# Sliding-window attention and a token/channel mixer on one core: the loads of v leave the place behind those of q and k and go behind the transposes of u

## The chip, the core and the metric

The kernel runs on one core of a Trainium2 chip. The core has five engines, each with a queue of its own that it works through in order: TensorE (matrix products, called PE in the profile), VectorE (DVE), ScalarE (ACT), GpSimd (POOL) and SyncE (SP, here used only to issue transfers). Sixteen DMA engines move data; the instructions that start them stand in the queues of SyncE, ScalarE and GpSimd. The metric is device time in microseconds of one execution, lower is better. Each number given for a kernel is the median of several runs.

## What is computed

Eight batches, eight heads, 576 positions, head size 64. Attention with a linear position bias and a causal window of 128, and then a mixer: two products over the positions, two over the channels.

```python
scores = scale * q @ k^T                      # (8, 8, 576, 576)
mask   = (rel >= 0) & (rel < 128)             # rel = query - key
scores = where(mask, scores - slope[h] * |rel|, -1e9)
x      = softmax(scores) @ v                  # heads side by side: (8, 576, 512)
h      = relu(x^T @ w_tok1) @ w_tok2          # over the 576 positions, width 256
u      = x + h^T
out    = u + relu(u @ w_ch1) @ w_ch2          # over the 512 channels, width 1536
```

Inputs and output are float32 in HBM; inside, the kernel works in bfloat16, and the loads that GpSimd issues cast on the way.

## The kernel before

The 576 positions of a batch are four chunks of 128 and a tail of 64; the tails of two batches are worked on together in the odd batch. Heads go in pairs. The work is cut into small functions with short names (lines 831 to 906), and the order in which they are issued is written out by hand in five strings. PROLOGUE, FIRST and SECOND cover the start and batches 0 and 1. PERIOD is issued for b = 2, 3, 4, 5 and 6, called rounds 2 to 6 here, and LAST for batch 7. A name with primes belongs to a later batch: S01'' in round b is a piece of batch b + 2. A name that a batch does not have is left out, so rounds 5 and 6 issue no loads of batch b + 3.

In a round the pieces are:

- `Lq'''`, `Lk'''`: loads of q and k of batch b + 3 into the buffers qn, qnt and kn, knt, five transfers each, issued by GpSimd (lines 188 to 211). There is one buffer for q and one for k, so a load waits until the transposes have read the batch before.
- `Zq''`, `Zk''`: DMA transposes of q and k of batch b + 2 from these buffers into qT and kT, two each, issued by SyncE (lines 217 to 221).
- `S..`: scores of eight blocks (six of batch b + 2 and two of b + 1): products on TensorE (lines 356 to 365), exponent on ScalarE (line 370), the product with the mask on VectorE (lines 376 to 385).
- `P0''` to `P4'`: probabilities times v on TensorE (lines 416 to 448), normalised by VectorE into x (lines 429 to 463).
- `v0'''` to `v4'''`: loads of v of batch b + 3 by GpSimd (line 213), into one of three buffers vp.
- `K`, `U`, `UT`: the two products over the positions, of batch b + 1 (lines 472 to 523); VectorE adds x and writes u (buffer ub, line 508).
- `X0'` to `X3'`: u turned. For batches 3 to 7 (`U_DMA`, line 19) X0 and X2 are DMA transposes of two chunks each on SyncE from ub into utb (lines 526 to 533), and X1 and X3 are empty. utb and ub have two buffers each.
- `C0` to `C11`: first product over the channels of batch b (line 548), which reads utb; `D..`: the second (line 607), each chunk added to u by VectorE (line 612) into one of four buffers ob and stored by SyncE (line 613). `T`, `E` and `Y` are the same for the tails, in odd batches.

The order around the change is thus set by three queues: GpSimd's, with Lq, Lk and v; SyncE's, with Zq, Zk, the stores and the X transposes; and TensorE's, which follows the string. In PERIOD the v loads stand between K0' and D20; as GpSimd has nothing else there, they are issued right after Lk'''.

Of the kernel before, what the change touches and what calls it, by code (L numbers as in the profile page):

```python
# [18 lines left out]
U_DMA = (3, 4, 5, 6, 7)  # L19
# [19 lines left out]
"""  # L39
PERIOD = """  # L40
Zq'' Lq''' C0 C7 T0 C6 C3 S31' S30' C4 P2' Zk'' Lk''' Y C10 C8 C9 P1' C2 T1 C1 P4' C11 P3' C5
K0' v4''' T2 K1' S01'' S00'' D00 v3''' v0''' D01 D02 U0' v1''' U3' UT' U2' U1' X1' P0'' v2'''
D20 D21 D10 X2' S10'' S11'' D11 X0' D22 D12 D30 D31 D32 S21'' S20'' X3' E0 E1 E2
"""
LAST = """
T1 C0 C1 T0 Y C11 C2 C10 T2 C7 C3 C8 C6 C5 C4 C9 D00 E0 D01 D02 E1 E2 D10 D30 D11 D20 D12 D31
# [16 lines left out]
def kernel(  # L63
# [11 lines left out]
    nc = tc.nc  # L75
    P = nc.NUM_PARTITIONS
# [6 lines left out]
    NC = S // P  # L83
# [11 lines left out]
    def T(name, shape, dt=bf16):  # L95
        return sb.tile(shape, dt, name=name, tag=name)
# [27 lines left out]
    i2 = T("i2", [P, ST])  # L124
    dist = T("dist", [P, 2, P], f32)
    distb = T("distb", [P, 2, P])
    sid = T("sid", [P, H, P])

    masks = T("masks", [P, 2, 2, 2, 2, P])
# [28 lines left out]
    utb = [T(f"utb{i}", [P, NC, NCB, P]) for i in range(2)]  # L158
# [54 lines left out]
    def load_v(b, c):  # L213
        t = vp[b % 3]
        load_tok(t[:, c, :, 0:D] if c < NC else None, t[0:ST, NC, :, 0:D], v, b, c)
# [188 lines left out]
    def pv(b, qb):  # L404
        vt = vp[b % 3]

        def f():
            psO = S2()
            for bank in range(2):
                o = psO[:, bank, :]  # L410
                first = True
                for hh in range(4):
                    h = bank * 4 + hh
                    ov = o[:, hh * (D + 1):(hh + 1) * (D + 1)]
                    if qb > 0:
                        nc.tensor.matmul(  # L416
                            ov, lhsT=prob(b, qb - 1, h, 1),
                            rhs=vt[:, qb - 1, h, 0:D + 1], start=first, stop=False)
                        first = False
                    nc.tensor.matmul(  # L420
                        ov, lhsT=prob(b, qb, h, 0),
                        rhs=vt[:, qb, h, 0:D + 1], start=first, stop=(hh == 3))
                    first = False
            ov = psO[:, :, 0:4 * (D + 1)].rearrange("p b (h e) -> p b h e", h=4)
            r = rt[qb % 2]
            rv = r[:, 0:H].rearrange("p (b h) -> p b h", b=2)

            def g():
                nc.vector.reciprocal(out=rv[:, :, :, None], in_=ov[:, :, :, D:D + 1])
                nc.vector.tensor_tensor(  # L430
                    out=xb[b % 2][:, qb, :].rearrange("p (b h d) -> p b h d", b=2, h=4),
                    in0=ov[:, :, :, 0:D],
                    in1=rv[:, :, :, None].broadcast_to([P, 2, 4, D]), op=ALU.mult)
            later(0, g)
        return f

    def pv_tail(b):
        vt = vp[b % 3]

        def f():  # L440
            psO = S2()
            E = 2 * (D + 1)
            for bank in range(2):
                for j in range(2):
                    hp = bank * 2 + j
                    o = psO[:, bank, j * E:(j + 1) * E]
                    for t in range(2):
                        nc.tensor.matmul(o, lhsT=prob_tail(b, t, hp),  # L448
                                         rhs=vt[:, NC - 1 + t, 2 * hp:2 * hp + 2, 0:D + 1],
                                         start=(j == 0 and t == 0), stop=(j == 1 and t == 1))  # L450

            def g():
                oa = psO[:, :, 0:2 * E].rearrange("p b (h e) -> p b h e", h=4)
                ra = rt[0][:, 0:H].rearrange("p (b h) -> p b h", b=2)
                nc.vector.reciprocal(out=ra[:, :, :, None], in_=oa[:, :, :, D:D + 1])
                for i in range(2):
                    ps = slice(i * D, (i + 1) * D)
                    ov = psO[ps, :, 0:2 * E].rearrange("p b (j i e) -> p b j i e", j=2, i=2)[:, :, :, i, :]
                    rv = rt[0][ps, 0:H].rearrange("p (b j i) -> p b j i", b=2, j=2)[:, :, :, i]
                    nc.vector.tensor_tensor(  # L460
                        out=xt[b % 2][ps, :].rearrange("p (b j i d) -> p b j i d", b=2, j=2, i=2)[:, :, :, i, :],
                        in0=ov[:, :, :, 0:D],
                        in1=rv[:, :, :, None].broadcast_to([D, 2, 2, D]), op=ALU.mult)
            later(0, g)
        return f
# [91 lines left out]
    def ch1_tail(b, g, n=4):  # L557
# [12 lines left out]
                                 func=ACT.Relu)  # L570
        return f

    def utail_trans(b):

        pi2 = (b // 2) % 2

        def f():
            nc.sync.dma_start_transpose(
                out=ut2[pi2][:, :, :], in_=utt[pi2][:, :, :, :].rearrange("p c i x -> p (c i x)"))
        return f  # L580
# [250 lines left out]
    def names(b):  # L831

        d = {}
        for kb in range(NC):
            for j in range(2):
                d[f"S{kb}{j}"] = score(b, kb, j)
        for qb in range(NC):
            d[f"P{qb}"] = pv(b, qb)
        d["P4"] = pv_tail(b)
        for i in range(2):  # L840
            d[f"K{i}"] = tok1(b, i)
        for c in range(NC):
            d[f"U{c}"] = tok2(b, c)
            d[f"X{c}"] = utrans(b, c)
        d["UT"] = tok2_tail(b)
        for ht in range(NHT):
            d[f"C{ht}"] = ch1(b, ht)
        if b % 2:
            for g in range(3):
                d[f"T{g}"] = ch1_tail(b, g)  # L850
            if b in Y_DMA:
                d["Y"] = utail_trans(b)
        for c in range(NC):
            for i, f in enumerate(ch2(b, c, CH2_PARTS)):
                d[f"D{c}{i}"] = f
        if b % 2:
            for i, f in enumerate(ch2_tail(b, CH2_PARTS)):
                d[f"E{i}"] = f
        for c in range(NC + 1):
            d[f"v{c}"] = lambda c=c: load_v(b, c)  # L860
        if b >= PE_BATCHES:
            d["Lq"], d["Lk"] = lambda: load_tokens(qn, qnt, q, b), lambda: load_tokens(kn, knt, k, b)
            d["Zq"] = lambda: dma_transpose(qT[b % 2], qn, qnt)
            d["Zk"] = lambda: dma_transpose(kT[b % 2], kn, knt)
        else:
            for nm, dst, src in (("q", qs, q), ("l", ks, k)):
                for hp in range(NHP):
                    d[f"{nm}{hp}"] = lambda dst=dst, src=src, hp=hp: load4(dst, src, b, hp)
                for hp in (0, 2):
                    d[f"{nm}{hp}{hp + 1}"] = lambda dst=dst, src=src, hp=hp: load4(dst, src, b, hp, 4)  # L870
            d["qt"] = lambda: load_qk_tail(b)
            for hp in range(NHP):
                d[f"A{hp}"] = pe_transpose(b, hp)
            d["AT"] = pe_transpose_tail(b)
        if b == 0:
            for hp in range(NHP):
                d[f"M{hp}"] = lambda hp=hp: mask_exps(hp)
                d[f"p{hp}"] = pv_hp(hp)
                d[f"k{hp}"] = tok1_hp(hp)
                d[f"u{hp}"] = tok2_hp(hp)  # L880
                d[f"x{hp}"] = utrans_hp(hp)
            for hp in range(2):
                d[f"q{hp}"] = lambda hp=hp: load_f32(nc.scalar, qf0, q, hp)
                d[f"l{hp}"] = lambda hp=hp: load_f32(nc.sync, kf0, k, hp)
                d[f"cq{hp}"] = lambda hp=hp: cast_f32(nc.vector.tensor_copy, qs, qf0, hp)
                d[f"ck{hp}"] = lambda hp=hp: cast_f32(nc.scalar.copy, ks, kf0, hp)
            d["LC"] = late_constants
            d["FC"] = first_constants
            d["e1"], d["e2"] = lambda: ones_v(1), lambda: ones_v(2)
            d["ek"], d["ex"] = fill_k1, fill_x1  # L890
            d["I"] = make_ident
            d["J"] = make_dist
            d["LW"] = load_w12
            d["B"] = make_bias
            d["O"] = lambda: ones_v(0)
            for kb in range(NC - 1):
                d[f"s{kb}"], d[f"t{kb}"] = score_half(kb, 0), score_half(kb, 1)
            for j in range(2):
                d[f"m{j}"] = lambda j=j: mask_tails(j)
            for g in range(3):  # L900
                d[f"G{g}"] = lambda g=g: load_wc1(g)
            for g in range(2):
                d[f"H{g}"] = lambda g=g: load_wc2(g)
            for n in range(1, 5):
                d[f"W{n}"] = warm(n)
        return d
# [46 lines left out]
```

The softmax here doesn't subtract the row's maximum and nothing guards it: scores larger than these inputs give would overflow.

## Time and profile before

| | us |
|---|---|
| median of 5 runs | 288.33 |
| lowest and highest of them | 287.83, 288.34 |
| the profiled execution's own time | 288.48 |
| its span, first to last instruction | 286.7 |
| TensorE busy (2535 products) | 280.4 (98%) |
| VectorE busy | 165.0 (58%) |
| ScalarE busy | 118.6 (41%) |
| GpSimd busy | 101.4 (35%) |

The busy time of TensorE is that of its matrix products; they are pipelined and their ends are modelled, so that a high share alone does not say that TensorE runs at its peak. Issuing a transfer occupies GpSimd for about 0.9 us for a load of four-dimensional shape such as v's; on SyncE such an issue is listed too, but is not counted as busy. The profile's table of DMA queues gives the share of the engines' time that the packets of a queue took: 81.9% for those that GpSimd issued over the whole span, 29.6% for those of SyncE. In a short stretch the sum of such shares can be above 1, since packets of several transfers are in flight together. From issue to landing a load of v takes 5.3 us (median), one of q or k 5.9, a transpose of u 3.3, the large one of q 3.9 and of k 3.8, and a store of line 613 2.1.

### The profile page before, as it was taken

What the parts mean: (1) busy time and instruction counts of PE and PEld (TensorE: products, weight loads), DVE (VectorE), ACT (ScalarE), POOL (GpSimd) and SP (SyncE); (2) the same over time, 40 slices, a digit from 0 to 9 for tenths busy, and PEclk for the clock granted to TensorE, in tenths of its full rate; (3) what the DMA queues carried; (4) which work ended last, traced back from release to release, by engine and by line L of the source; (5) the groups of instructions that cost most, each with busy time, mean ns of one, the idle gap of its engine ahead of it and who ended that gap; (6) DMA issues with size and microseconds to landing.
All of it is one profiled execution on the core that took longest, in us unless ns stands there. A gap on an engine that the chain in (4) does not pass through costs nothing.

```text
span 286.7 us, 6128 instructions
## 1 busy us (share of the span) xinstructions
PE 280.4 (98%) x2535; PEld 155.4 (54%) x2535; DVE 165.0 (58%) x329; ACT 118.6 (41%) x182; POOL 101.4 (35%) x132
## 2 busy tenths in 40 slices
PE   8999999999999999999999999999999999999995
PEld 3577546464565556545664456545664456455452
DVE  5359766537668376745556666745556667523222
ACT  3898941148515443326542343326542343104300
POOL 8997443099199029501960008800000000000000
PEclk9999999999999999999999999999999999999999
DMA  8999999799999989987998269998404310052032
GB/s 195 166 198 194 205 177 136 165 164 146 149 206 191 157 210 108 155 166 187 137 155 131 110 122 165 154 167 169 83 2 110 112 37 2 37 146 57 0 92 93
DMA packets 150267, 38.38 MB, mean 134 GB/s; under 512 B 137440, under 2 KB 145760, under 8 KB 150240
## 3 DMA queue, kind: packets, MB, share of 16 engines
q0 software_dynamic: 103152, 17.41, 81.9%
q1 hardware_dynamic: 46544, 20.06, 29.6%
q10 hardware_dynamic: 544, 0.52, 0.5%
q8 instruction: 20, 0.33, 0.5%
q14 instruction: 7, 0.06, 0.0%
HBM read 35.85 MB, written 9.44 MB: 158 GB/s over the span
## 4 chain that ended last, share of the span: by engine, by line
PE 94%; ACT 3%; DVE 1%; issue 1%; DVEq 0%
PE psM L548 29%; PE psM L607 29%; PE psM L506 4%; PE psM L481 4%; PE psT L565 4%; PE psS L356 4%; PE psM L629 4%; PE psS L420 2%; PE psS L416 2%; PE psT L750 2%; PE psS L448 1%; PE psM L588 1%; PE psS L360 1%; PE psM L234 1%; PE psM L490 1%; ACT kT L239 1%
## 5 line engine op out<-in xcount | busy, mean ns | idle before, releaser
L548 PE MATMUL psM<-utb,WC 128*128 128x512 bf16 x384 | 90.8, 379 | 0.0
L607 PE MATMUL psM<-WC,r 128*128 128x512 bf16 x372 | 86.3, 379 | 0.0
L370 ACT ACTIVATE pe<-psS 128x1024 bf16<-128x1024 f32 x56 | 54.6, 1024 | 38.0 <-PE psS L356 34.4
L607 PEld LDWEIGHTS <-r 128*128 128x128 bf16 x372 | 34.4, 98 | 40.1 <-issue 3.1
L548 PEld LDWEIGHTS <-WC 128*128 128x128 bf16 x384 | 34.6, 98 | 36.3 <-issue 1.5
L376 DVE TENSOR_TENSOR pb<-pe,masks 128x1024 bf16<-128x1024 bf16 x42 | 29.0, 691 | 26.3 <-ACT pe L370 26.2
L554 ACT ACTIVATE r<-psM 128x512 bf16<-128x512 f32 x48 | 28.5, 599 | 35.5 <-PE psM L548 35.4
L190 POOL DMA_DIRECT2D qn<-in_q_dram x24 | 21.1, 903 | 60.0 <-DMA qT<-qn 59.5
L551 DVE TENSOR_SCALAR r<-psM 128x512 bf16<-128x512 f32 x48 | 32.7, 687 | 15.7 <-PE psM L548 15.5
L612 DVE TENSOR_TENSOR ob<-psM,ub 128x512 f32<-128x512 f32 x31 | 21.0, 688 | 27.4 <-PE psM L607 27.3
L190 POOL DMA_DIRECT2D vp<-in_v_dram x32 | 28.8, 930 | 0.5 <-PE psM L506 0.3
L190 POOL DMA_DIRECT2D kn<-in_k_dram x24 | 21.2, 916 | 17.2 <-DMA kT<-kn 11.7
L430 DVE TENSOR_TENSOR xb<-psS,rt 128x512 bf16<-128x512 f32 x28 | 19.4, 691 | 1.0
L508 DVE TENSOR_TENSOR ub<-psM,xb 128x512 bf16<-128x512 f32 x28 | 17.5, 683 | 2.6 <-PE psM L506 2.6
L568 ACT ACTIVATE r2t<-psT 128x512 bf16<-128x512 f32 x12 | 7.2, 600 | 24.8 <-PE psT L565 24.8
L420 PEld LDWEIGHTS <-pb 128*128 128x128 bf16 x224 | 13.5, 97 | 4.3 <-issue 1.0
L420 PE MATMUL psS<-vp,pb 128*128 128x65 bf16 x224 | 15.6, 193 | 0.0
L506 PE MATMUL psM<-r,W 128*128 128x512 bf16 x56 | 14.5, 379 | 0.5 <-DVE ob L612 0.5
L499 ACT ACTIVATE r<-psM 128x512 bf16<-128x512 f32 x7 | 4.2, 596 | 25.0 <-PE psM L490 25.0
L481 PE MATMUL psM<-xb,W 128*128 128x256 bf16 x112 | 13.4, 273 | 0.0
L356 PE MATMUL psS<-qT,kT 64*128 64x256 bf16 x168 | 13.2, 271 | 0.0
L565 PEld LDWEIGHTS <-WC 128*128 128x128 bf16 x192 | 11.6, 98 | 2.2
(134 smaller groups left out, 302.6 us busy)
## 6 DMA issues: line engine op xcount, KB each, us to landing
out_dram<-ob SPq DMA_DIRECT2D x31, 256.0 KB, 2.1
vp<-in_v_dram POOLq DMA_DIRECT2D x32, 128.0 KB, 5.3
kn<-in_k_dram POOLq DMA_DIRECT2D x24, 128.0 KB, 5.9
qn<-in_q_dram POOLq DMA_DIRECT2D x24, 128.0 KB, 5.9
WC<-in_moe_w_ch_dram POOLq DMA_DIRECT2D x3, 512.0 KB, 9.0
WC<-in_moe_w_ch_dram POOLq DMA_DIRECT2D x2, 768.0 KB, 14.3
out_dram<-ob SPq DMA_DIRECT2D x10, 128.0 KB, 2.3
qs<-in_q_dram POOLq DMA_DIRECT2D x3, 256.0 KB, 6.4
```

The source lines that it names most:

```text
L190: nc.gpsimd.dma_start(out=dst, in_=src[b, :, c * P:(c + 1) * P, :].rearrange("h s d -> s h d"))
L356: nc.tensor.matmul(s[h][:, a * 256:(a + 1) * 256], lhsT=kT[i][r, kb, hp, :], rhs=qT[i][r, kb:kb + 2, hp, :], start=True, stop=True)
L370: nc.scalar.activation(out=e[:, h, :], in_=s[n][:, None, :] if split else t2[:, :, :], func=ACT.Exp, scale=scale)
L376: nc.vector.tensor_tensor(out=p[:, :].rearrange("p (h x) -> p h x", h=2), in0=e[:, :, :], in1=masks[:, j].rearrange("p h g a x -> p h (g a ...
L420: nc.tensor.matmul(ov, lhsT=prob(b, qb, h, 0), rhs=vt[:, qb, h, 0:D + 1], start=first, stop=(hh == 3))
L481: nc.tensor.matmul(st["t"][h][:, dh * 256:(dh + 1) * 256], lhsT=W1[:, c, dh * P:(dh + 1) * P], rhs=by_half(xb[b % 2][:, c, :])[:, h], star ...
L506: nc.tensor.matmul(t[:, :], lhsT=W2[:, j, c * P:(c + 1) * P], rhs=r1[b % 2][:, j, :], start=(j == 0), stop=(j == 1))
L548: nc.tensor.matmul(t[:, :], lhsT=WC1[:, cb, ht * P:(ht + 1) * P], rhs=utb[b % 2][:, :, cb, :], start=(cb == 0), stop=(cb == NCB - 1))
L551: nc.vector.tensor_scalar(out=r2[b % 2][:, ht, :], in0=t[:, :], scalar1=0.0, scalar2=None, op0=ALU.max)
L554: nc.scalar.activation(out=r2[b % 2][:, ht, :], in_=t[:, :], func=ACT.Relu)
L565: nc.tensor.matmul(psT[:, j * P:(j + 1) * P], lhsT=WC1[:, cb, ht * P:(ht + 1) * P], rhs=utt[pi2][:, cb, :, :], start=(j == 0 and cb == 0), ...
L607: nc.tensor.matmul(t[:, :], lhsT=r2[b % 2][:, ht, c * P:(c + 1) * P], rhs=WC2[:, ht, :], start=(ht == 0), stop=(ht == NHT - 1))
```

## The change

In PERIOD the five loads of v are taken out of their places and put, in the order v4, v3, v0, v1, v2, behind X0' and a new piece R'. R is a copy on GpSimd of two elements a partition, one from the part of utb that X0 writes and one from the part that X2 writes, into a new small buffer `hold` that nothing reads. GpSimd therefore waits at R' until both transposes of u of batch b + 1 have landed, and issues the loads of v of batch b + 3 after that. The order of the other pieces is as before; of PROLOGUE, FIRST, SECOND and LAST nothing is changed. Rounds 5 and 6 get R' too, with no load behind it.

```diff
 PERIOD = """
 Zq'' Lq''' C0 C7 T0 C6 C3 S31' S30' C4 P2' Zk'' Lk''' Y C10 C8 C9 P1' C2 T1 C1 P4' C11 P3' C5
-K0' v4''' T2 K1' S01'' S00'' D00 v3''' v0''' D01 D02 U0' v1''' U3' UT' U2' U1' X1' P0'' v2'''
-D20 D21 D10 X2' S10'' S11'' D11 X0' D22 D12 D30 D31 D32 S21'' S20'' X3' E0 E1 E2
+K0' T2 K1' S01'' S00'' D00 D01 D02 U0' U3' UT' U2' U1' X1' P0'' D20 D21 D10 X2' S10'' S11'' D11
+X0' R' v4''' v3''' v0''' v1''' v2''' D22 D12 D30 D31 D32 S21'' S20'' X3' E0 E1 E2
 """
@@
     distb = T("distb", [P, 2, P])
+    hold = T("hold", [P, 2])
     sid = T("sid", [P, H, P])
@@
+    def behind_u(b):
+
+        def f():
+            nc.gpsimd.tensor_copy(out=hold[:, :], in_=utb[b % 2][:, 0:NC:2, 0, 0])
+        return f
+
     def utail_trans(b):
@@
+        if b in U_DMA:
+            d["R"] = behind_u(b)
         for c in range(NC):
             for i, f in enumerate(ch2(b, c, CH2_PARTS)):
                 d[f"D{c}{i}"] = f
```

## The prediction

> **What bounds the kernel now.** I read the table of stretches first, one stretch for each round of the loop (cut where TensorE starts a round's first matmul of line 548), then TensorE's waits, then the queues of GpSimd and SyncE in order of time, then the transfers.
>
> ```profile
> 100.45:129.97 29.52, 29.52 (x250) 15.51 (x248) 19.16 (x37) 10.27 (x15) 12.58 (x15) 1.00 1.57 161
> 129.97:164.96 34.99, 34.99 (x309) 19.53 (x310) 20.96 (x39) 15.59 (x21) 12.58 (x15) 1.00 1.30 142
> 164.96:194.47 29.51, 29.51 (x250) 15.51 (x248) 18.74 (x35) 10.26 (x15) 12.57 (x15) 1.00 1.40 155
> 194.47:229.47 35.00, 35.00 (x311) 19.53 (x310) 20.98 (x39) 15.60 (x21) 0.00 (x0) 1.00 0.40 92
> 229.47:257.17 27.70, 27.70 (x219) 14.49 (x218) 14.90 (x28) 6.38 (x10) 0.00 (x0) 1.00 0.22 57
> ```
>
> The columns are the stretch, its length, then busy time of TensorE's matmuls, its weight loads, VectorE, ScalarE and GpSimd, then the granted clock, the DMA share and GB/s. These are rounds 2 to 6. TensorE is busy for 156.72 of 156.72 us, at a granted clock of 1.00. A busy figure of pipelined matmuls could hide a bubble, so the second reading matters more. Round 5 has no load of q, k or v at all (GpSimd 0.00; batch 8 doesn't exist), and takes 35.00 us; round 3 has all fifteen and takes 34.99. Rounds 2 and 4, both with loads, take 29.52 and 29.51. What the loads do beside TensorE is worth at most 0.01 us a round as things stand.
>
> ```profile
> PE psT L750 <- DVE zt L745: 1.0, 1, 1.0
> PE psM L506 <- DVE ob L612: 0.5, 1, 0.5
> PE psM L234 <- DVE qT L239: 0.4, 1, 0.4
> PE psM L739 <- DVE ub L732: 0.2, 1, 0.2
> PE psM L259 <- DVE kT L239: 0.2, 1, 0.2
> ```
>
> That is every wait of TensorE: 2.3 us, none on a DMA, and in the rounds that the change touches none at all (the table left nothing over). The chain that ended last is TensorE for 94% of the span.
>
> ```profile
> 114.60 0.71 POOL L193 DMA_DIRECT2D vp<-in_v_dram  x1
> 115.27 3.55 POOL L190 DMA_DIRECT2D vp<-in_v_dram  x4
> 135.10 3.50 POOL L190 DMA_DIRECT2D qn<-in_q_dram  x4 [16.28 <-DMA qT<-qn]
> 121.23 2.87 SPq L528 DMA_TRANSPOSE utb<-ub  x2
> 127.31 3.20 SPq L613 DMA_DIRECT2D out_dram<-ob  x3
> 130.73 1.73 SPq L218 DMA_TRANSPOSE qT<-qn  x1
> 133.94 1.32 SPq L218 DMA_TRANSPOSE kT<-kn  x1
> ```
>
> GpSimd's queue, then SyncE's (start, length, line, what). In round 2 v of batch 5 is issued from 114.60 to 118.82, right behind q and k; then GpSimd stands for 16.28 us until q's transpose of the next round has landed. The transposes of u go out at 121.23.
>
> ```profile
> 118.00:120.00 2.00, 2.00 (x22) 1.08 (x20) 1.92 (x4) 0.11 (x2) 0.82 (x1) 1.00 2.43 155
> 120.00:122.00 2.00, 2.00 (x18) 1.05 (x17) 1.97 (x6) 0.31 (x1) 0.00 (x0) 1.00 2.43 156
> 124.00:126.00 2.00, 2.00 (x13) 0.90 (x10) 0.70 (x2) 1.94 (x2) 0.00 (x0) 1.00 0.89 196
> 126.00:128.00 2.00, 2.00 (x11) 0.92 (x10) 1.88 (x3) 0.00 (x0) 0.00 (x0) 1.00 0.00 0
> ```
>
> The DMA share (last but one) holds at 2.43 while the fifteen loads drain, past the start of u's transposes, and is 0.00 from 126: u is turned by then, and the engines are free just where v would now go.
>
> **The change part by part.** Its three sets of v loads (batches 5, 6, 7, in rounds 2, 3, 4) move behind R'; R' itself runs in rounds 2 to 6.
>
> *Removed from the early place:* five issues, 0.71 + 3.55 = 4.26 us of GpSimd and their traffic. From round 3's start of loads at 135.10 the share stays near 2.4 until about 151.5, 16.4 us for three tensors, so 5.5 us of full DMA for v. u's transposes meet less of it: a pair issued at 185.74 in round 4 landed 5.1 us (median) after issue, that at 153.63 in round 3 3.1 us. Gain there up to 2.0 us a round, on the path 0: C0 reads u's transpose at 129.97, 164.96 and 194.47, and TensorE waited at none of them, with u turned by 126, 158 and 191.5. Were this cover gone (u over 3 us later in round 4), a late u would be paid one for one.
>
> *R' added:* no GpSimd copy is in the trace. The nearest rows are its fills of 128x1 at 0.10 us and of 128x40 at 0.30 to 0.38, and the select over 128x256 at 0.41. Two elements a partition is nearest to 0.10; range 0.10 to 0.41, five times, so 0.5 to 2.05 us of GpSimd, on the path 0. What queues behind R' on GpSimd is only v, then q of the next round, and that waits for Zq, which is queued on SyncE behind these same u transposes and three stores, so R' is always released first (126.0 against 135.10; 158 against 172.81). New also is that a later transpose into the same u buffer, two rounds on, has to wait for R': done some 60 us before.
>
> [...]
>
> *v later:* R' at about 126.1, 158.1 and 191.6, issues 4.26 us, landing 5.3 us after (the page's median for v), so v is there by 135.7, 167.7 and 201.2. The first reader is P0'' one round on: 153.06 for batch 5, 185.10 for batch 6, and by the same offset of 23.1 us into the round, 217.6 for batch 7. Margin 16 to 17 us; cost 0. Without the margin each late microsecond would count.
>
> *What v runs beside now:* the three stores of line 613, which land in 2.1 us (5.3 at most) and whose buffers are not rewritten for 20 us (the next product of line 612 comes near 151), and the transposes Zq and Zk. Of v's 5.5 us of traffic some is done before Zq starts: in round 3 v starts 4.6 us before 130.73, in round 4 9.0 us before 167.08, in round 5 3.6 us before 195.24. What is left to push Z back is 0.9, 0 and 1.9 us if v drains as fast as before, 5.5 each if none of it is served before Z. A near precedent: the transpose of q at 72.55, with loads just issued, released GpSimd after 6.5 us; that at 130.73, with none, after 4.4. So I take 2 us later in rounds 3 and 5, 0 in round 4; ends 0 and 5.5.
>
> *Who waits for that:* S01'' reads k's transpose. It lands at 133.94 + 3.7 = 137.6 for a reader at 147.85 (margin 10.2); in round 4 at 171.08 + 3.8 = 174.9 for 180.06 (5.2, or 3.8 if the reader waits for the tail transpose too, 172.78 + 3.5); in round 5 at 198.18 + 4.7 = 202.9 for 212.36 (9.5). All hold against 2 us; against 5.5 only round 4 gives, by 0.3 or 1.7. Next, q's loads of round 3 start at 135.1 + 2 (5.5 at most), and q and k drain in 11 us: 148 to 151.6, where all three tensors now end at 151.5. u's next transposes start at 153.63, so nothing reaches them.
>
> **Sum**, against the profiled execution: its own 288.48 us are 286.7 of span and 1.78 around it; 0 (u earlier) + 0 (R') + 0 (v later) + 0 (Z later by 2) = 288.5. That execution lies 0.15 over the median of 288.33, so the forecast for the median is 288.3.
>
> **The rivals.**
> A, faster: a bubble behind C0 that busy time doesn't show, from u's crowded transposes in round 4. Price: all 2.0 us of the difference between 5.1 and 3.1, 286.3. For it: the share shows u's transposes beside loads. Against: round 4 is no longer than round 2, and no wait on a DMA is recorded.
> B, slower: v pushes k's transpose past its reader in round 4. It decides once Zk is over 3.8 us late there, priced with the whole 5.5: 1.7 us, 290.0. For it: v and the transposes use the same engines, and that is the tightest margin. Against: v has 9.0 us of lead there for 5.5 us of traffic.
> C, it doesn't do what it says: R' awaits only one of the two transposes, or the loads leave GpSimd no later than now. Then less moves than above, and the time is 288.3 again.
>
> **How the numbers follow.** Five runs span 287.83 to 288.34, so about 0.2% (0.58 us) is what a measurement of this kernel can tell from no change. The forecast, with C in it, gets 0.85; A 0.06; B 0.09. Of the 0.85 some 0.04 falls out of the band on either side by the spread of medians. So faster 0.10, same 0.77, slower 0.13. The likeliest case's own range is 287.8 to 288.9; to hold 8 in 10 I reach a little beyond on both sides, 287.7 to 289.0.
>
> **What would show it.** Right: rounds 2 to 6 again take 29.5, 35.0, 29.5, 35.0 and 27.7 us with TensorE full; v's issues stand at about 126, 158 and 190 behind a GpSimd copy under 0.5 us that waits for the u transposes; round 4's u transposes land in about 3 us, not 5; GpSimd's wait for qT in round 3 ends by 137 to 138. Wrong: a wait of TensorE on kT near 180 (B), a round shorter than before (A), or a round that stretches with no wait on a DMA, which nothing here foresees.

## The result, and the profile after

| | before | changed |
|---|---|---|
| median, us | 288.12 (56 runs) | 288.80 (32 runs) |
| lowest | 287.73 | 288.10 |
| highest | 288.69 | 293.23 |
| ratio | | 1.0028, 95% interval 1.0019 to 1.0036 |
| the profiled execution's own time | 288.48 | 291.6 |
| its span | 286.7 | 289.7 |

The change costs 0.28% by the ratio, some 0.8 us (0.7 between the medians), and its runs scatter far more. The profiled execution of the changed kernel is one of its long ones, 2.8 us over the median; it shows the loss enlarged, and is read here for where it lies.

First the table of stretches again, cut at the changed kernel's own round starts (columns as before the prediction):

```profile
103.45:132.96 29.51, 29.51 (x249) 15.50 (x248) 19.16 (x37) 10.26 (x15) 11.40 (x15) 1.00 1.39 138
132.96:167.96 35.00, 35.00 (x310) 19.51 (x310) 20.98 (x39) 15.60 (x21) 14.13 (x18) 1.00 1.42 147
167.96:197.47 29.51, 29.51 (x249) 15.49 (x248) 18.75 (x35) 10.27 (x15) 12.11 (x16) 1.00 1.32 147
197.47:232.47 35.00, 35.00 (x310) 19.53 (x310) 20.97 (x39) 15.60 (x21) 0.83 (x2) 1.00 0.72 113
```

Rounds 2 to 5 take 29.51, 35.00, 29.51 and 35.00 us, against 29.52, 34.99, 29.51 and 35.00. Round 6, to the first product of that line in batch 7, takes 28.43 in both (229.47 to 257.90, and 232.47 to 260.90). All of the rounds that the change edits are as long as they were. But round 2 begins at 103.45 instead of 100.45: the loss is complete before the first instruction that the diff adds or moves. TensorE's waits, the three longest:

```profile
PE psS L357 <- DMA kT<-kn: 2.3, 1, 2.3
PE psM L235 <- DVE qs L830: 1.7, 2, 1.5
PE psT L757 <- DVE zt L752: 1.0, 1, 1.0
```

The first is new: scores (line 357, which was 356) wait 2.3 us for the transpose of k. The chain that ended last says when, as start, length, what. First the kernel before, then the changed one:

```profile
82.66 1.75 PE psM L481 x16
84.41 0.32 PE psM L490 x4
84.73 0.44 PE psS L356 x8
```

```profile
80.26 7.26 DMA kT<-kn
87.51 0.05 issue
87.56 0.61 PE psS L357 x8
```

Before, TensorE comes to these scores of batch 3 (in round 1, from the string SECOND) straight from other products. In the changed kernel the chain leaves TensorE: SyncE starts k's transpose at 80.26, it lands 7.26 us later, and only then do the scores run. The second wait, at the start, goes back to the first load of q (buffers qf and qs). Three more profiles below show a wait for such a load there, of 1.3, 1.3 and 0.3 us, one of them with no buffer moved, and at 75 us TensorE was only 0.5 us behind. So of the 3.0 us 0.5 are from there and 2.3 are the wait for k; the last 0.2 lie in the scores themselves, whose eight products take 0.61 us after the wait and 0.44 without it.

What the change meant to do, it does. GpSimd's queue and then SyncE's, around rounds 2 and 3:

```profile
129.63 0.19 POOL L577 COPY hold<-utb 128x2 bf16<-128x2 bf16 x1 [11.61 <-DMA utb<-ub]
130.14 0.68 POOL L194 DMA_DIRECT2D vp<-in_v_dram  x1 [0.33 <-PE psM L614]
130.81 3.52 POOL L191 DMA_DIRECT2D vp<-in_v_dram  x4
143.90 3.50 POOL L191 DMA_DIRECT2D qn<-in_q_dram  x4 [9.57 <-DMA qT<-qn]
```

v goes out behind the copy, and the copy behind u's transposes. Those of round 4, which landed 5.1 us after issue, land after 3.2 (medians of two).

So the question is what in the diff can make a transpose late at 80 us, when all that it adds or moves among the instructions comes after 100. The queues of the two kernels hold the same instructions up to there. One thing differs from the first instruction on: where the buffers lie. `hold` has 4 bytes a partition, and gets a slot of 32, between distb and sid. The byte address in a partition, from the two built programs:

| buffer | before | changed |
|---|---|---|
| sid | 26880 = 105 x 256 | 26912, 32 past |
| qn, qnt, kn, knt | 74752 = 292 x 256, and so the other three | 74784, 32 past |
| qT, kT, vp | multiples of 256 | 32 past |
| ub, utb | 192 past | 224 past |

### The profile page after: what moved, and what is told of

Its sections match the earlier page's. It is cut to its first block, busy times and chain, and to the rows that moved or that the text cites. A ratio compares the mean times of both kernels' runs of the same rounds, so it can differ in the third digit from the quotient of the medians.

```text
span 289.7 us, 6140 instructions
## 1 busy us (share of the span) xinstructions
PE 279.3 (96%) x2535; PEld 154.8 (53%) x2535; DVE 165.6 (57%) x329; ACT 118.8 (41%) x182; POOL 102.3 (35%) x137
## 4 chain that ended last, share of the span: by engine, by line
PE 89%; DMA 4%; ACT 3%; DVE 1%; issue 1%; SPq 1%; ACTq 0%; DVEq 0%
PE psM L549 29%; PE psM L614 27%; PE psM L507 4%; PE psT L566 4%; PE psS L357 4%; PE psM L636 4%; PE psM L482 4%; DMA kT<-kn 3%; PE psS L421 2%; DMA qf<-in_q_dram 2%; PE psS L417 2%; PE psS L449 1%; PE psM L595 1%; PE psS L361 1%; PE psM L491 1%
## 5 line engine op out<-in xcount | busy, mean ns | idle before, releaser
L549 PEld LDWEIGHTS <-WC 128*128 128x128 bf16 x384 | 34.6, 98 | 36.3 <-issue 1.5
L577 POOL COPY hold<-utb 128x2 bf16<-128x2 bf16 x5 | 0.9, 186 | 88.2 <-DMA utb<-ub 79.3
```

The costliest lines, as they stand in the source:

```text
L549: nc.tensor.matmul(t[:, :], lhsT=WC1[:, cb, ht * P:(ht + 1) * P], rhs=utb[b % 2][:, :, cb, :], start=(cb == 0), stop=(cb == NCB - 1))
```

## The experiments

Three theories for the loss. T1: the moved addresses make early transfers slower. T2: the new place of v's loads. T3: the copy itself. Each "before" below is the median of the runs of the kernel before that were taken along with the experiment on the same chip.

**hold alone.** The kernel before, plus the buffer:

```diff
     distb = T("distb", [P, 2, P])
+    hold = T("hold", [P, 2])
     sid = T("sid", [P, H, P])
```

> The kernel before with the 4-byte buffer hold added at the place where the change adds it, used by nothing. Its slot of 32 bytes moves every buffer behind it by 32 bytes, from a multiple of 64 to 32 past one; the instructions are those of before. T1 (the moved addresses make the early loads and transposes slower, and k's transpose at 80 us is then late for its reader): slower by 0.2 to 0.4%, as the whole change (1.0028), with single runs of 1 to 3 us more. T2 (the place of v's loads costs it, in rounds 2 to 5): the same as before, ratio 0.999 to 1.001. T3 (the copy itself or the end of the program costs it): the same as before.

Measured: 288.76 against 288.43, ratio 1.0039 (1.0008 to 1.0071); 292.3 and 292.7 among its eleven runs. Four bytes that nothing uses cost what the change costs. Its wait, in the list of TensorE's waits, is the same one:

```profile
PE psS L357 <- DMA kT<-kn: 1.1, 1, 1.1
```

**The change with hold behind all other buffers.**

```diff
-    hold = T("hold", [P, 2])
     sid = T("sid", [P, H, P])
...
     ob = [T(f"ob{i}", [P, DM], f32) for i in range(4)]
+    hold = T("hold", [P, 2])
```

> The changed kernel with hold put behind all other buffers, so that every other buffer has its address of before. T1: the same as before, ratio 0.999 to 1.001. T2: slower by 0.2 to 0.4%, as the whole change. T3: slower by 0.2 to 0.4%.

Measured: 288.55 against 288.43, ratio 1.0002 (0.9993 to 1.0011). No wait on kT. T2 falls, and so does T3 as the source of the 0.28%, since the copy is in this kernel too.

**R' alone**, hold behind all other buffers, v where it was:

```diff
-D20 D21 D10 X2' S10'' S11'' D11 X0' D22 D12 D30 D31 D32 S21'' S20'' X3' E0 E1 E2
+D20 D21 D10 X2' S10'' S11'' D11 X0' R' D22 D12 D30 D31 D32 S21'' S20'' X3' E0 E1 E2
```

> The kernel before with R' added behind X0' and hold behind all other buffers; v's loads stay where they were. T1: the same as before, ratio 0.999 to 1.001. T2: the same as before. T3: slower by 0.1 to 0.4%; the copy's own time by the trace is 5 times 0.19 us, all while GpSimd has nothing else.

Measured: 288.55 against 288.43, ratio 1.0006 (0.9997 to 1.0014): not told from no change. A small part of T3 is left all the same, some 0.2 us outside the span, which the last section takes up.

**hold of 64 bytes**, the changed kernel otherwise:

```diff
-    hold = T("hold", [P, 2])
+    hold = T("hold", [P, 32])
...
-            nc.gpsimd.tensor_copy(out=hold[:, :], in_=utb[b % 2][:, 0:NC:2, 0, 0])
+            nc.gpsimd.tensor_copy(out=hold[:, 0:2], in_=utb[b % 2][:, 0:NC:2, 0, 0])
```

> The changed kernel with hold of 64 bytes a partition in its place, so that the buffers behind it move by 64 bytes and stay on multiples of 64. T1 in its narrow form (32 past a multiple of 64 is what costs): the same as before, ratio 0.999 to 1.001. T1 in a wide form (a multiple of 256 is needed, which the buffers ahead of the small ones had before): slower by 0.2 to 0.4%. T2 and T3: slower by 0.2 to 0.4%.

Measured: 288.59 against 288.43, ratio 1.0012 (1.0001 to 1.0023), two of eleven runs over 289.5. By its time it lies between the two forms, below the 0.2% of the wide one; the transposes decide for the wide one. SyncE's queue for the first four near 50 us, when few other transfers are in flight (packets of GpSimd's take 10.0% of the DMA engines' time from 49 to 57 us, and 7.0% from 49.5 to 58), in the kernel before and then in the changed one (start, length of the issue):

```profile
50.18 1.74 SPq L218 DMA_TRANSPOSE qT<-qn  x1
52.03 1.19 SPq L221 DMA_TRANSPOSE qT<-qnt  x1
53.33 1.60 SPq L218 DMA_TRANSPOSE kT<-kn  x1
55.02 1.21 SPq L221 DMA_TRANSPOSE kT<-knt  x1
```

```profile
50.81 2.31 SPq L219 DMA_TRANSPOSE qT<-qn  x1
53.23 1.37 SPq L222 DMA_TRANSPOSE qT<-qnt  x1
54.71 1.77 SPq L219 DMA_TRANSPOSE kT<-kn  x1
56.58 1.78 SPq L222 DMA_TRANSPOSE kT<-knt  x1
```

In sum 5.74 us before and 7.23 changed; 7.17 with hold alone, 7.20 with 64 bytes; 5.86 with hold last and 5.72 with R' alone. This sum is a cleaner sign than the time, since it barely scatters. It splits T1: T1a, the address that a transpose writes; T1b, the address that it reads; T1c, the addresses that the loads write.

**Only what the transposes write, 32 past** (the kernel before; `pa` and `pb_` are not used):

```diff
+    pa = T("pa", [P, 16])
     qT = [T(f"qT{i}", [P, NC + 1, NHP, P]) for i in range(2)]
     kT = [T(f"kT{i}", [P, NC + 1, NHP, P]) for i in range(2)]
+    pb_ = T("pb_", [P, 112])
```

> The kernel before with 32 unused bytes ahead of the buffers qT and kT and 224 behind them: what the DMA transposes of q and k write stands 32 past a multiple of 256, all other buffers keep their place within 256 bytes. T1a (the address that a transpose writes costs): the first four transposes near 50 us take 7.1 to 7.3 us of SyncE's issue in sum, as with all buffers moved (7.23 and 7.17), not 5.7 to 5.9; the time is slower by 0.2 to 0.4%. T1b (the address that a transpose reads) and T1c (the addresses that the loads write): 5.7 to 5.9, and the time of before, ratio 0.999 to 1.001.

Measured: 288.43 against 288.34, ratio 1.0001 (0.9993 to 1.0010), sum 5.72. T1a falls.

**Only what the transposes read, 32 past:**

```diff
+    pa = T("pa", [P, 16])
     qn = T("qn", [P, NC, DM])
...
     knt = T("knt", [ST, DM])
+    pb_ = T("pb_", [P, 112])
```

> The kernel before with 32 unused bytes ahead of qn, qnt, kn and knt and 224 behind them: what the loads of q and k from batch 2 on write, and the transposes read, stands 32 past a multiple of 256. T1b: the first four transposes take 7.1 to 7.3 us in sum, and the time is slower by 0.2 to 0.4%. T1a: 5.7 to 5.9, and the time of before. T1c: the transposes 5.7 to 5.9, the loads of q and k up to 72 us land later than the 5.3 to 5.7 us (median) of before, and the time is slower by about half of 0.3%.

Measured: 288.62 against 288.34, ratio 1.0017 (0.9996 to 1.0039), so by its time alone unclear, with 291.96 among twelve runs. The transposes are clear: SyncE's queue shows in them the same lengthening as with all buffers moved.

```profile
50.48 2.09 SPq L220 DMA_TRANSPOSE qT<-qn  x1
52.69 1.54 SPq L223 DMA_TRANSPOSE qT<-qnt  x1
54.33 1.81 SPq L220 DMA_TRANSPOSE kT<-kn  x1
56.23 1.76 SPq L223 DMA_TRANSPOSE kT<-knt  x1
```

7.20 in sum; from issue to landing 4.4, 2.6, 4.4 and 2.9 us, where the kernel before has 3.9, 2.3, 3.8 and 2.4. These buffers are also what the loads of q and k write, but the loads are not slowed: issued from 20 to 72 us, those of q land after 5.2 us and those of k after 7.2 (medians of eight), against 5.2 and 6.9 in the kernel before, and after 5.2 and 6.9 with the offset of 128 tried below. The wait of TensorE for k is there too, 0.5 us:

```profile
PE psM L236 <- DMA qs<-in_q_dram: 1.3, 1, 1.3
...
PE psS L358 <- DMA kT<-kn: 0.5, 1, 0.5
```

**All the others, 32 past** (`pa` of 32 bytes ahead of sid, 224 ahead of qn, 32 ahead of vp):

```diff
+    pa = T("pa", [P, 16])
     sid = T("sid", [P, H, P])
...
+    pb_ = T("pb_", [P, 112])
     qn = T("qn", [P, NC, DM])
...
+    pc = T("pc", [P, 16])
     vp = [T(f"vp{i}", [P, NC + 1, H, VROW]) for i in range(3)]
```

> The kernel before with all buffers from sid on moved by 32 bytes except qn, qnt, kn, knt, qT and kT, which keep their place within 256 bytes. T1a and T1b: the transposes of q and k take 5.7 to 5.9 us in sum near 50 us, and the time is that of before, ratio 0.999 to 1.001. T1c: slower by 0.15 to 0.4%, with transposes as before and loads of v, q and k that land later.

Measured: 288.36 against 288.34, ratio 0.9999 (0.9991 to 1.0008), sum 5.79. With the loads of q and k as read above, T1c falls.

**What the transposes write, 128 past**, a single profiled execution, with the diff for writing but `[P, 64]` twice:

> As with 32 bytes ahead of qT and kT, but 128 (and 128 behind): one look, at the transposes. T1a with a step of 128 bytes: 5.7 to 5.9 us for the first four transposes. T1a with a step of 256: 7.1 to 7.3. T1b, T1c: 5.7 to 5.9.

Measured: 5.74 in sum, one time of 287.72. It told nothing new once T1a had fallen.

**What they read, 128 past**, with the diff for reading but `[P, 64]` twice:

> The kernel before with qn, qnt, kn and knt moved to 128 past a multiple of 256. T1b with a step of 128 bytes: 5.7 to 5.9 us for the first four transposes, and the time of before. T1b with a step of 256: 7.1 to 7.3 us, and slower by 0.1 to 0.4%.

Measured: 7.24 in sum; 288.59 against 288.31, ratio 1.0013 (1.0002 to 1.0024). A step of 128 is not enough: 32, 64 and 128 past a multiple of 256 lengthen the issues alike (7.20, 7.20 and 7.24).

**The changed kernel with only the reading buffers put right:**

```diff
     hold = T("hold", [P, 2])
...
+    pa = T("pa", [P, 112])
     qn = T("qn", [P, NC, DM])
```

> The changed kernel, hold in the place where the change has it, and 224 unused bytes ahead of qn, so that qn, qnt, kn and knt stand on multiples of 256 again. T1b (the address that a transpose reads is the whole cost): the first four transposes near 50 us take 5.7 to 5.9 us in sum (7.23 in the changed kernel), no wait of TensorE on kT near 85 us, and the time of before, ratio 0.999 to 1.001. If something else in the change costs it: still slower by 0.2 to 0.4%.

Measured: 5.74 in sum, no wait on kT; 288.37 against 288.31, ratio 1.0003 (0.9994 to 1.0012). The loss is gone.

**The changed kernel with hold last, and only the reading buffers put wrong** (the diff for reading, 32 bytes, on top of hold last):

> The changed kernel with hold behind all other buffers (288.55 against 288.43) and only qn, qnt, kn and knt moved to 32 past a multiple of 256. T1b: the transposes near 50 us take 7.1 to 7.3 us in sum, and the time is slower by 0.1 to 0.4%, with single runs of 1 us and more over the median. If the reading address costs nothing beside the transposes themselves: 7.1 to 7.3 us, and ratio 0.999 to 1.001.

Measured: 7.16 in sum; 288.74 against 288.31, ratio 1.0020 (1.0004 to 1.0036), five of twelve runs over 289. The loss is back.

**The changed kernel with hold last and u's buffers put on a multiple of 256 too:**

```diff
+    pa = T("pa", [P, 32])
     xb = [T(f"xb{i}", [P, NC, DM]) for i in range(2)]
```

> The changed kernel with hold behind all other buffers and 64 unused bytes ahead of xb, so that u's buffers ub (192 past a multiple of 256 before) stand on multiples of 256 as well as those of q and k. T1b: u's transposes land in 2.7 to 2.9 us instead of 3.1 to 3.3. As TensorE waited for none of them, the time stays that of before, ratio 0.999 to 1.001; if u's lateness did cost something unseen, it is faster by 0.1 to 0.3%.

Measured: 288.38 against 288.31, ratio 1.0004 (0.9995 to 1.0013). The same shows in another buffer: the list of transfers for rounds 2 to 6, with u's buffers 192 past (hold last) and then at a multiple of 256 (count, median us from issue to landing):

```profile
utb<-ub SPq DMA_TRANSPOSE x10, 3.2
```

```profile
utb<-ub SPq DMA_TRANSPOSE x10, 2.8
```

0.4 us sooner, and worth nothing, since TensorE never waited for it. In the kernel with hold of 64 bytes u's buffers come to stand on a multiple of 256 as well (192 + 64), and there it is 2.8 too; in the twelve other profiles it is 3.1 to 3.3. None of these versions that ran more than once beats the kernel before.

Taken together: with the reading buffers of q and k off a multiple of 256, 17 of 58 timed runs of the experiments are over 289 us (and 12 of the 32 of the changed kernel); with them on it, none of 66, and none of the kernel before. The medians of the five move by 0.16 to 0.43 us; their intervals are wide because of the single long runs. With only the reading buffers off the ratios are 1.0013 to 1.0020, with all buffers 32 past they are 1.0028 and 1.0039. The intervals overlap, so whether the other buffers add something once the reading ones are off stays open; by themselves they cost nothing (0.9999).

## Why the prediction was wrong, step by step

**The step that failed** is the list of what the change adds. It costed R', the moved issues and their traffic, and took "0 (R')" for the whole of the addition. The buffer that R' needs was shown in the diff, and was not among the terms. It moves what the transposes of q and k read, and their issues near 50 us then take 1.5 us more for the set of four (7.2 against 5.7). In the profile with only the reading buffers moved the sets of rounds 3, 4 and 5 take 1.4, 1.1 and 1.0 us more than in the kernel before; other transfers are in flight there, so these figures scatter.

Whether that reaches the end depends on the stage before the loop, where the prediction had looked least: it read the rounds from 100 us on, as the diff edits only PERIOD. There the transposes and loads feed each other with little to spare: the loads of k wait for the transposes to release kn, and the next transposes wait for the loads. In the kernel before, then in the changed one (GpSimd's loads of k, then SyncE's next transposes of q and k):

```profile
57.61 3.50 POOL L190 DMA_DIRECT2D kn<-in_k_dram  x4 [11.68 <-DMA kT<-kn]
72.55 3.45 SPq L218 DMA_TRANSPOSE qT<-qn  x1
77.39 1.33 SPq L218 DMA_TRANSPOSE kT<-kn  x1
```

```profile
59.61 3.50 POOL L191 DMA_DIRECT2D kn<-in_k_dram  x4 [13.20 <-DMA kT<-kn]
76.00 2.86 SPq L219 DMA_TRANSPOSE qT<-qn  x1
80.26 2.14 SPq L219 DMA_TRANSPOSE kT<-kn  x1
```

GpSimd gets to the loads of k at 57.25 to 58.19 us in the eight profiles with the reading buffers on a multiple of 256, and at 58.72 to 59.61 in the six with them off it. The next set of transposes then starts at 72.05 to 73.65 in the first, and at 73.60 to 76.00 in the second. In the kernel before, k's transpose lands 5.1 us after its issue, at 82.5, for a reader at 84.57: 2.1 us to spare. In the eight profiles 0.9 to 2.3 us are to spare. In the six, three have 0 to 0.7 us left, and in the other three TensorE waits, with k landing at 85.3 (twice) and 87.5. The executions with the wait took 289.19, 289.29 and 291.60 us, the three without it 288.18 to 288.34. So the margin is used up in some executions and not in others, and that is where the scatter comes from as far as the profiles show; the runs that were only timed have no trace.

The second term taken as unchanged is the time around the span, 1.78 us. It is 0.2 longer in every kernel with the copy (last section), so a small part of the 0.7 to 0.8 us is the copy's.

None of the signs came by which the prediction would know itself wrong: the wait on kT is in round 1, not near 180 us, and no round grew or shrank. That 288.80 still lies within its 287.7 to 289.0 is luck, since nothing in its sum or its rivals led there.

**What bounds the kernel**: right for the rounds, which kept their lengths to 0.01 us. The last cut of the first table, at 257.17, stands at a product of line 565 and not of line 548, which starts at 257.90; round 6 is 28.43 us long and not 27.70.

**u earlier, worth 0**: right in both, 5.1 to 3.2 us in round 4, and 1.0002 with hold last.

**R' at 0.10 us, range 0.10 to 0.41**: 0.18 to 0.19 in the changed kernel. Two of the 34 copies with a row in the seven profiles that have it fall outside the range, and both start within a product of VectorE with two inputs in SBUF. VectorE's and GpSimd's rows in round 5 of the kernel with hold last:

```profile
222.71 0.69 DVE L377 TENSOR_TENSOR pb<-pe,masks 128x1024 bf16<-128x1024 bf16 x1 [0.22 <-ACT pe L371]
222.72 0.73 POOL L577 COPY hold<-utb 128x2 bf16<-128x2 bf16 x1 [27.69 <-DMA utb<-ub]
```

The copy starts 0.01 us after a product with two inputs in SBUF and ends 0.05 after it, at 0.73 instead of 0.19. With hold of 64 bytes another, started 0.22 us into such a product, takes 0.51 and ends 0.04 after it. In the seven profiles ten copies start within such a product with 0.1 us or more of it left, and all ten end 0.04 to 0.06 us after it. Five start within a sum of VectorE that reads one input from PSUM (line 619 here), and take 0.18 to 0.19. Why a copy ends only behind such a product was not shown. It costs nothing here, as forecast.

**R' at 126.1, 158.1 and 191.6, and v right behind it**: with hold last the copies stand at 126.74, 158.10 and 190.33, v's issues 0.5 us behind; right. v lands later than forecast: the last two loads of the first set, issued by 131.4, take 10.0 us (median), not 5.3, so they are there at about 141 and not at 135.7. Its reader comes at 152.8, so the cost of 0 holds.

**Z later by 2 us in rounds 3 and 5, 0 in round 4, ends 0 and 5.5**: right for round 4, and right that the margins hold, but too small for the other two. From the list of transfers in round 3, with hold last and then in the kernel before (us to landing):

```profile
qT<-qn SPq DMA_TRANSPOSE x1, 11.2
...
kT<-kn SPq DMA_TRANSPOSE x1, 6.2
```

```profile
qT<-qn SPq DMA_TRANSPOSE x1, 3.8
...
kT<-kn SPq DMA_TRANSPOSE x1, 3.7
```

k's transpose lands at 137.49 + 6.2 = 143.7, not 137.6, so 6.1 us later, past the end of 5.5, and in round 5 at 200.80 + 7.0 = 207.8, not 202.9, 4.9 later. Of margins of 10.2 and 9.5 some 4 are left. In round 4 it lands at 171.11 + 3.9 = 175.0, against 174.9. The bound of 5.5 took v's traffic to drain at its own rate and the transposes to wait for the rest; the traces show both slowed: q's transpose lands after 11.2 us instead of 3.8, v's last two loads after 10.0 instead of 5.3. The loads of q then start at 142.36, not 135.10, where the prediction had named 137 to 138 as its sign. Rival B had put the late transpose into round 4, where it is not late; in rounds 3 and 5 the margin holds. It is not what cost the time.

**Which address costs.** The runs agree in two things: reading matters and writing does not (7.20 against 5.72 us for the set of four), and any offset tried costs (7.20, 7.20 and 7.24 at 32, 64 and 128). The issues show no difference by the size of the offset. With the reading buffers moved by 224 bytes from 32 past to the next multiple of 256 (qn from 74784 to 75008 = 293 x 256) the set takes 5.74. Why a transpose takes longer when it reads off such a multiple was not shown.

## What to carry to other kernels

A diff that adds a buffer moves all buffers behind it (here four bytes moved them by 32): list their addresses before and after, and count that as a part of the change, with a price in every stage that uses them, the ones that the diff does not touch too. Keep what a DMA transpose reads on a multiple of 256 bytes (here the issues of a set of four took 5.7 to 5.9 us there, and 7.2 at 32, 64 and 128 past; put small buffers last), and when a loss shows up ahead of the first changed instruction, try the allocation alone first. A margin of 2 us in a stage where loads and transposes wait for each other is one that 1.5 us more on one set of transposes can use up in some runs, so look at the spread of runs and not only at the median.

## What the runs showed of the hardware that was not expected

A DMA transpose from SBUF that reads 32, 64 or 128 bytes past a multiple of 256 took 4.3 to 4.4 instead of 3.7 to 3.8 us to land for 512 KB of k (16 blocks of 128 columns a partition), and 3.2 instead of 2.8 for half of that at 192 past, where what it writes was moved along; where it wrote 32 past alone, nothing changed (3.9 us for q and 3.7 for k). Loads that wrote 32 past cost nothing either (0.9999, 0.9991 to 1.0008).

Loads issued by GpSimd and transposes issued by SyncE landed later when they were in flight together: a transpose of q that took 3.8 us in round 3 of the kernel before took 9.1 to 11.2 in that of the six kernels with v behind u, and the last two loads of v's first set took 10.0 (median, hold last), where the median of all loads of v in the kernel before is 5.3. Three stores are in flight there as well, so the price of the loads alone is not separated.

A kernel with the GpSimd copy has more time around the span: 1.90 to 2.04 us in all 99 timed runs of the seven that have it (mean 1.97), and 1.72 to 1.84 in all 58 of the six experiments without it (mean 1.77). The 0.2 us are more than the 0.06 to 0.17 us that the ratios of 1.0002 to 1.0006 stand for in the four kernels that have the copy and the reading buffers in place, but within their intervals. Whether it is the copy as such, or that GpSimd's last instruction now comes late, was not tried.
